# One zero fill moved behind the w_down stores and gate/up loads in five FFN blocks

## Chip, cores and metric

The kernel runs on one core of a Trainium2 chip. Its time is the device time of that core in microseconds, as the median of several executions; below, profiles give a span of one execution, which starts with the first instruction and is a little shorter.

## What is computed

The kernel computes one decode step of a transformer block, forward and backward. `c` gives six modulation vectors; `x` goes through a modulated layer norm, attention over the last 4096 positions of a long cache, a second modulated layer norm and a gated FFN. The outputs are the new `x` and the gradients of all inputs.

```python
W = min(4096, max(256, Sk // 4))          # Sk is 65536
k = jnp.repeat(k_cache[:, :, Sk - W:, :], rep, axis=1)
v = jnp.repeat(v_cache[:, :, Sk - W:, :], rep, axis=1)
...
h = _sigmoid(g) * u
return jnp.einsum('bsf,fd->bsd', h, w_down)
...
x = x + gb * _B_ref(h, B_w_gate, B_w_up, B_w_down)
```

Two of the gradients, those of `k_cache` and `v_cache`, have the shape of the whole cache (4 x 65536 x 128 each). Only their last 4096 positions are not zero, so the rest has to be filled with zeros in device memory. That is most of what the kernel writes.

## The kernel before

The kernel is written out by hand in one order (`manual_schedule`), and each engine runs its own instructions in that order. Work goes in stages: load the modulation weights and the cache, attention forward, the matrices that the attention gradients need, the FFN, and at last all the gradients that hang on the FFN's result.

**The zero fills.** The zero region of the two cache gradients is cut into pieces of [128, 4096] elements, 1 MB each. `zero(n)` (L147 on) takes the next n of them off a list and issues each as one DMA from GpSimd (L169; a few narrower ones are issued in two parts, L162 and L165). A fill has no input but a tile of zeros that stays in SBUF, so it can be placed anywhere. The tables at the head of the file (`Z_...`) say how many fills go to which place; they are spread over the whole kernel, among the transfers that carry data.

**Queues.** GpSimd issues the fills, the stores of weight gradients and the loads of the gate and up weights, all through one software queue (q0 in the profile), and waits at each for what that transfer depends on. A GpSimd DMA also takes one of eight semaphores in turn, so it waits for the landing of the eighth GpSimd DMA before it. SyncE issues the loads of w_down through a queue of its own (q1).

**The FFN.** F = 3584 is done in `NB` = 7 blocks q of 512 columns. A block holds the gate and up weights in a tile of two halves (j = 0 to 3 and 4 to 7), double buffered by q % 2, and w_down in one tile `wd_v` of two halves s. In block q:

- VectorE, for each j, multiplies the weights by the gradient of gate/up and sums (`ttr`, L210, into `dh2acc`), and ScalarE overwrites the same tile with the weight gradient (`outer_act`, L241). In between PE and ScalarE transpose pieces of w_o and v for later (`side`, L836 and L837).
- After j = 3 the first half of the weight gradient is stored (`store_ug(q, 0, 4)`, L868, two DMAs of 512 KB), after j = 7 the second half (`store_ug(q, 4, 4)`).
- Then PE and ScalarE compute the gate and up values of block q + 1 (`front`, `gates`), VectorE reduces its two w_down halves (`wd_ttr`, L210 into `junk`) and overwrites them with the gradient (`wd_outer`, L206), which is stored from the same place (`store_wd`, L854).
- `load_ug(q + 2, ...)` (L864) fetches the gate/up weights of block q + 2 into the half that `store_ug(q, ...)` has emptied, so it waits for that store's landing. `load_wd(q + 2, s)` (L851, SyncE) likewise waits for the landing of `store_wd(q + 1, s)`, and `wd_ttr(q + 2, s)` waits for the load.
- At the end of the block `dug_part` (L989, L990) makes the gradient of gate/up for the next block.

`Z_FFN` has four numbers per block: fills after the first gate/up store, after the second, after the first w_down store (and the first load), and after the second load.

Of the kernel before, what the change touches and what calls it, by code (L numbers as in the profile page):

```python
# [52 lines left out]
Z_N = spread(31, 128)  # L53
Z_B = [n + (i in (31, 38)) for i, n in enumerate(spread(29, 43))] + [1, 1, 1, 1, 0] + [1, 1, 0, 1, 1, 0, 1, 1] + [1, 0, 1, 0, 1, 0, 0, 0]
Z_FOLD = (1, 1, 3)
Z_FFN = [(1, 1, 0, 1)] * 5 + [(1, 1, 1, 2), (1, 2, 1, 0)]
Z_END = (1, 2, 1, 0, 0)
@with_exitstack
def kernel(
# [956 lines left out]
    for q in range(NB):  # L1016
        z = Z_FFN[q]
        more = q + 1 < NB
# [315 lines left out]
```

## Time and profile before

| what | value |
|---|---|
| time, median of 3 | 599.43 us (599.01 to 601.42) |
| profiled span | 598.7 us |
| bytes by DMA | 246.64 MB, of which HBM written 185.60 MB and read 60.30 MB |
| busiest engine | PE 411.2 us (69%), then VectorE 326.6, ScalarE 284.9, GpSimd 163.1 |
| DMA | 9 tenths busy in all slices but the first (8) and the last (6) |
| the FFN | about 319 to 480 us, one block some 22 to 25 us |

Read it from the DMA row: the sixteen DMA engines hardly rest. The time of a span can only fall if fewer bytes move, if they move faster, or if a stretch in which too little was queued is filled. For a change of order, look at single stretches of the FFN: the GB/s of each, what GpSimd waits for before an issue, and how long VectorE waits for a w_down load.

### The profile page before, as it was taken

To read this page: it belongs to the slowest core of one execution; us is meant where nothing else is said; L and a number is where in the kernel's file an instruction comes from. 1 tells how busy PE (TensorE), PEld (TensorE's weight loads), DVE (VectorE), ACT (ScalarE), POOL (GpSimd) and SP (SyncE) were. 2 spreads that over 40 slices of the span, in tenths; PEclk is the share of its full clock that TensorE was granted. 3 is DMA by queue.
4 is the path that set the end of the run, shared out by engine and by line. 5 is a ranking of instruction groups with operands and counts; after the bars stand their busy time and mean duration, and the time that the engine had idled before them with its cause. 6 is when DMAs were issued, how large, how long until landed. Compare 5 with 4: busy or idle time off the path is not lost.

```text
span 598.7 us, 11068 instructions
## 1 busy us (share of the span) xinstructions
PE 411.2 (69%) x4612; PEld 275.3 (46%) x4612; DVE 326.6 (55%) x620; ACT 284.9 (48%) x429; POOL 163.1 (27%) x262
## 2 busy tenths in 40 slices
PE   3997689999999989999984435534445196766300
PEld 3995334334344545546664334433344166565300
DVE  3654499999511010160007495694777888768530
ACT  2489514567211014213225665864867866873200
POOL 0003123222223212222232244333343253122330
PEclk9999699999999999999995555555555586755555
DMA  8999999999999999999999999999999999999996
GB/s 349 419 418 422 413 425 412 427 421 425 427 419 426 422 428 423 422 421 424 423 397 407 421 411 415 411 411 412 379 403 412 424 416 414 420 424 425 424 415 269
DMA packets 45027, 246.64 MB, mean 412 GB/s; under 512 B 5085, under 2 KB 5085, under 8 KB 24544
## 3 DMA queue, kind: packets, MB, share of 16 engines
q0 software_dynamic: 38832, 216.55, 94.7%
q1 hardware_dynamic: 6096, 29.37, 12.5%
q8 instruction: 36, 0.59, 0.4%
q14 instruction: 15, 0.12, 0.1%
q10 hardware_dynamic: 48, 0.01, 0.0%
HBM read 60.30 MB, written 185.60 MB: 411 GB/s over the span
## 4 chain that ended last, share of the span: by engine, by line
PE 40%; DMA 26%; DVE 19%; ACT 7%; issue 4%; ACTq 0%; POOLq 0%; SPq 0%; DVEq 0%
PE b_ps L691 17%; DMA out_dram<-arena 16%; DMA arena<-in_B_w_down_dram 6%; PE n_ps L636 6%; DVE junk L210 5%; DVE arena L210 4%; DVE arena L193 4%; DVE arena L206 4%; DMA arena<-in_B_w_gate_dram 3%; ACT arena L241 3%; PE t_ps L598 2%; PE tp_wq L453 2%; PE w_ps L394 2%; PE tp_k L434 1%; PE fold_ps L875 1%
## 5 line engine op out<-in xcount | busy, mean ns | idle before, releaser
L169 POOL DMA_DIRECT2D out_dram<-zeros x114 | 62.0, 545 | 200.4 <-PE q_ps L471 50.7
L691 PE MATMUL b_ps<-arena 128*128 128x512 bf16 x512 | 116.2, 379 | 0.0
L836 PE MATMUL tp_side<-ident_bf,arena 128*128 128x128 bf16 x432 | 51.7, 300 | 46.6 <-ACT arena L837 39.7
L837 ACT COPY arena<-tp_side 128x1024 bf16<-128x1024 bf16 x54 | 53.9, 1012 | 50.7 <-PE tp_side L836 50.4
L193 DVE TENSOR_TENSOR arena<-arena 128x2048 bf16<-128x2048 bf16 x64 | 76.5, 1223 | 2.3 <-PE n_ps L636 0.3
L691 PEld LDWEIGHTS <-arena 128*128 128x128 bf16 x512 | 48.8, 98 | 55.8 <-issue 2.9
L210 DVE CUSTOM_DVE_ANT_0 arena<-arena,scr 128x1024 bf16<-128x1024 bf16 x56 | 65.2, 1219 | 10.4 <-ACT scr L990 10.4
L636 PE MATMUL n_ps<-arena 128*128 128x512 bf16 x256 | 65.7, 378 | 6.2 <-DVE arena L193 4.6
L836 PEld LDWEIGHTS <-arena 128*128 128x128 bf16 x432 | 43.0, 139 | 51.2 <-issue 50.9
L241 ACT ACTIVATE arena<-scr,h 128x1024 bf16<-128x1024 bf16 x56 | 61.5, 1146 | 1.4 <-DVE dh2acc L210 1.3
L636 PEld LDWEIGHTS <-arena 128*128 128x128 bf16 x256 | 24.6, 97 | 41.6 <-issue 16.2
L210 DVE CUSTOM_DVE_ANT_0 junk<-arena,b1k 128x1024 bf16<-128x1024 bf16 x28 | 34.2, 1222 | 10.1 <-DMA arena<-in_B_w_down_dram 9.6
L1161 ACT ACTIVATE arena<-ps_kv 128x512 bf16<-128x512 f32 x48 | 26.1, 680 | 26.8 <-PE ps_kv L1157 26.5
L868 POOL DMA_DIRECT2D out_dram<-arena x28 | 21.1, 760 | 63.9 <-ACT arena L241 44.9
L202 DVE CAST arena<-b_ps 128x512 bf16<-128x512 f32 x6 | 4.1, 691 | 61.6 <-PE b_ps L691 61.6
L600 ACT CAST arena<-t_ps 128x512 bf16<-128x512 f32 x56 | 30.1, 589 | 12.1 <-PE t_ps L598 12.1
L1157 PE MATMUL ps_kv<-junk,arena 8*128 8x128 bf16 x256 | 27.1, 303 | 10.9 <-DVE arena L206 9.5
L1157 PEld LDWEIGHTS <-arena 8*128 8x128 bf16 x256 | 25.1, 139 | 12.6 <-issue 12.6
L455 ACT COPY arena<-tp_wq 128x1024 bf16<-128x1024 bf16 x23 | 21.8, 1032 | 8.1 <-PE tp_wq L453 8.1
L970 PE MATMUL fg<-hh_bf,arena 128*128 128x1 bf16 x224 | 8.2, 166 | 20.7 <-DMA arena<-in_B_w_down_dram 17.8
L877 ACT CAST arena<-fold_ps 128x512 bf16<-128x512 f32 x16 | 9.4, 588 | 24.1 <-PE fold_ps L875 24.1
L655 ACT ACTIVATE arena<-n_ps 128x512 bf16<-128x512 f32 x8 | 4.3, 594 | 33.1 <-PE n_ps L652 33.1
(299 smaller groups left out, 652.8 us busy)
## 6 DMA issues: line engine op xcount, KB each, us to landing
out_dram<-zeros POOLq DMA_DIRECT2D x114, 1024.0 KB, 14.6
out_dram<-arena POOLq DMA_DIRECT2D x32, 1024.0 KB, 17.1
out_dram<-arena POOLq DMA_DIRECT2D x50, 512.0 KB, 9.7
arena<-in_A_wq_dram SPq DMA_DIRECT2D x8, 1024.0 KB, 20.4
arena<-in_A_wo_dram POOLq DMA_DIRECT2D x8, 1024.0 KB, 11.9
arena<-in_w_mod_dram POOLq DMA_DIRECT2D x7, 1024.0 KB, 18.1
arena<-in_B_w_down_dram SPq DMA_DIRECT2D x14, 512.0 KB, 8.9
arena<-in_B_w_up_dram POOLq DMA_DIRECT2D x14, 512.0 KB, 9.9
```

Of the source, the lines that this page charges most:

```text
L169: ins = nc.gpsimd.dma_start(out=region.bitcast(FP32), in_=zeros[:, :])
L193: return nc.vector.tensor_tensor(out=out, in0=a, in1=b, op=op)
L206: return nc.vector.tensor_scalar(out=out, in0=a, scalar1=s1, scalar2=None, op0=op0)
L210: return nc.vector.tensor_tensor_reduce(out=out, in0=w, in1=b, scale=1.0, scalar=0.0, op0=ALU.mult, op1=ALU.add, accum_out=acc)
L241: return nc.scalar.activation(out=out, in_=b, func=ACT.Copy, scale=col)
L600: nc.scalar.copy(out=o, in_=ps)
L636: mm = nc.tensor.matmul(nbank[k][:, :], lhsT=k_nat[:, g, t_ * DH:(t_ + 1) * DH], rhs=vp[:, t_ % 2, 4 * k:4 * k + 4, :].rearrange("p h d -> ...
L691: mm = nc.tensor.matmul(bbank[p][k][:, :], lhsT=a4[:, p, h, :], rhs=wo_t[u][:, a, k * 512:(k + 1) * 512], start=(i == 0 and a == 0), stop= ...
L836: nc.tensor.transpose(tp[:, i * P:(i + 1) * P], blk[:, i * P:(i + 1) * P], ident_bf[:, :])
L837: nc.scalar.copy(out=blk if dst is None else dst, in_=tp[:, :])
L1157: nc.tensor.matmul(ps[:, t4 * DH:(t4 + 1) * DH], lhsT=rows[32 * g:32 * g + HG, t_ * P:(t_ + 1) * P], rhs=hd[32 * g:32 * g + HG, :], start= ...
L1161: nc.scalar.activation(out=o, in_=ps[:, :], func=ACT.Copy, scale=float(scale))
```

## The change

In blocks 0 to 4, the fill that stood after the second gate/up store is issued at the end of the block instead, behind the w_down stores and the loads of gate and up, where one fill stood already. It brings those stores and loads forward in GpSimd's queue by one fill, and leaves two fills in a row before the next block's first store. Blocks 5 and 6 and the number of fills stay.

```diff
-Z_FFN = [(1, 1, 0, 1)] * 5 + [(1, 1, 1, 2), (1, 2, 1, 0)]
+Z_FFN = [(1, 0, 0, 2)] * 5 + [(1, 1, 1, 2), (1, 2, 1, 0)]
```

The order of GpSimd's DMAs in one of these blocks:

```
before   store A   zero   store B   zero   load A   store w0   store w1   load B   zero
after    store A   zero   store B          load A   store w0   store w1   load B   zero   zero
```

(A and B are the halves of the gate/up tile, w0 and w1 those of w_down.)

## Prediction

> **What bounds the kernel now.** I read the page's DMA rows first, then the stage table, then the chain of waits, then GpSimd's timeline around the moved fill.
>
> ```profile
> DMA packets 45027, 246.64 MB, mean 412 GB/s; under 512 B 5085, under 2 KB 5085, under 8 KB 24544
> q0 software_dynamic: 38832, 216.55, 94.7%
> q1 hardware_dynamic: 6096, 29.37, 12.5%
> ```
>
> These are the page's DMA rows. All 40 slices but the first and the last stand at 9 tenths of DMA time, and no compute engine is above 69%. 246.64 MB in 598.7 us is a kernel that waits for transfers. Nearly all of them go through q0, which GpSimd fills in program order; q1 (SyncE) carries the w_down loads in the stage concerned.
>
> The stage table (columns: stretch in us, its length, busy us of PE, PEld, DVE, ACT and POOL, clock, DMA share, GB/s) has a stretch long before the FFN, then the FFN in steps of 23 us, about one block each:
>
> ```profile
> 160.00:280.00 120.00, 115.61 (x885) 60.82 (x883) 22.88 (x57) 24.16 (x35) 28.91 (x51) 1.00 1.13 423
> 343.00:366.00 23.00, 10.40 (x160) 8.88 (x158) 16.18 (x35) 16.31 (x18) 9.60 (x14) 0.50 1.07 413
> 366.00:389.00 23.00, 11.40 (x168) 9.80 (x166) 17.02 (x37) 16.23 (x18) 8.66 (x14) 0.50 1.07 412
> 389.00:412.00 23.00, 9.63 (x138) 8.08 (x136) 15.12 (x32) 16.45 (x18) 8.93 (x14) 0.50 1.07 409
> 412.00:435.00 23.00, 10.28 (x160) 9.10 (x160) 16.08 (x31) 14.34 (x15) 7.44 (x11) 0.50 1.10 392
> 435.00:458.00 23.00, 10.91 (x163) 9.39 (x161) 16.36 (x35) 17.32 (x22) 9.00 (x13) 0.50 1.06 406
> ```
>
> The FFN moves 409 to 413 GB/s in ordinary blocks, and less in two. The finer windows say where:
>
> ```profile
> 420.00:424.00 4.00, 2.05 (x16) 1.73 (x17) 2.60 (x10) 1.55 (x3) 2.48 (x4) 0.50 0.99 382
> 424.00:428.00 4.00, 1.32 (x12) 1.15 (x12) 4.00 (x7) 4.00 (x5) 0.16 (x1) 0.50 0.98 324
> 428.00:432.00 4.00, 0.99 (x11) 0.83 (x10) 3.90 (x8) 4.00 (x5) 1.98 (x3) 0.50 1.11 415
> ```
>
> That is the only real hole: (412-382)/412 x 4 + (412-324)/412 x 4 = 0.29 + 0.85 = 1.1 us.
>
> The chain of waits, in order of time, shows why compute was late there:
>
> ```profile
> 369.84 10.08 DMA out_dram<-arena
> 379.98 7.70 DMA arena<-in_B_w_down_dram
> 405.01 12.62 DMA arena<-in_B_w_down_dram
> 417.65 1.22 DVE junk L210
> ```
>
> A w_down store has to land before the next w_down load may use its tile; that load has to land before VectorE goes on. Here one load took 12.62 us against 7.70, VectorE started only at 417.65, and the next gate/up store came so late that the queue thinned. The loop of store, load, compute is in the chain, yet DMA runs at its usual rate in every other block: it has about the length of the block's transfers and does not limit by itself.
>
> **What the Trainium skill says.** "DMA: Bandwidth & Descriptors", section "Issuing engines are not separate DMA queues": all DMAs share 16 engines and interleave. The trace agrees: total GB/s stays near 412 while q1 runs beside q0. The same page, section "Queues, rings and completion order", says each engine takes its queues in turn by packets, and "Anatomy of one DMA — SWDGE (gpsimd) path" says the engines never wait on semaphores; the issuing sequencer does, and holds all behind it. The trace agrees with that too: GpSimd's issues stand in program order with gaps before those that wait for ACT, VectorE or a landing. No page gives a price for fill order.
>
> **The change, part by part.** Call the halves of a gate/up store A and B, the loads into the same halves U and V, the w_down stores w0 and w1, a 1 MB fill Z. One block on GpSimd was A Z B Z U w0 w1 V Z; it becomes A Z B U w0 w1 V Z Z. No instruction of PE, ACT, VectorE or SyncE changes, and fills keep their order, so none is added or lost.
>
> 1. Bytes. Per block A, B, U and V move 1 MB each, the w_down stores 1 MB, the w_down loads 1 MB on q1, fills 3 MB: 9 MB (9.44e6 bytes) at 412 GB/s is 22.9 us. Unchanged, so the floor under a block is unchanged.
>
> 2. GpSimd time. Fills cost 545 ns each on GpSimd (the row of L169). The same number is issued: 0.
>
> 3. The fill removed from behind B. U waits for A's landing, V for B's. A's place in the stream is unchanged: two fills follow V before the next A where one did, but one fewer stood earlier. So U is issued when it was. What has changed is what lies in q0 while GpSimd stands there: Z and B, 2 MB or 5.1 us, instead of 3 MB and 7.6 us. In the profile U's two issues stand at 391.69 and 392.89 with 2.56 and 0.44 us of wait before them. 5.1 us is still more than the longest such wait (4.5 us, once). Cost: 0, with up to 5.1 - 4.5 = 0.6 us of slack left.
>
> 4. U, w0, w1, V sit one fill earlier in q0. 1.05 MB / 412 GB/s = 2.5 us sooner each. The w_down loads hang on w0 and w1, so they start up to 2.5 us sooner. VectorE waits 9.6 us in five times for these loads (3.8 at most), so nearly all of each early wait goes. But this is compute time, hidden: from one copy of dug (422.6) to the next (444.5) a block without such waits takes 21.9 us of compute, and its transfers 22.9. Compute reaches the end of the FFN some 2.5 us earlier; the bytes do not. Worth 0 directly.
>
> 5. Two fills behind V, ahead of the next A. A waits for ACT's first half of outer products; this is the place of the hole (V and its fill issued by 423.6, A at 430.02). The fill adds 2.5 us of queued work exactly there, more than the 1.1 us lost, and step 4 makes A's data come sooner. Gain up to 1.1 us. The next stretch (406 against 412: 0.3 us) may gain as well.
>
> 6. Overlap. A w_down load now runs beside V, Z, Z rather than V, Z, A. If fills take a larger share than stores do, the load lasts longer; between the quick and the slow loads of the chain (7.70 and 12.62 us) lies 4.9, most of which is the one bad case. I take 1 us, covered by the 2.5 of step 4.
>
> Sum: 0 to -1.4 us. The slow load at 405 may be an accident of this one execution (DMA share rises to 1.39 just then, in one window of 4 us), so I take -0.8: 599.4 - 0.8 = 598.6 us.
>
> **The rivals.**
> - Hidden (599.4 us): the hole belongs to the profiled execution, or comes back elsewhere. For it: the transfer total is unchanged and the queue full in four of six stretches. Against it: the added fill sits just where the queue thinned.
> - Faster (about 594.3 us): the order itself lifts the rate, as loads and stores lie closer and compute is no longer late. If the 138 us of the FFN (mean 407 GB/s of the six stretches from 320 to 458) ran at the 423 of the stretch before, 138 x (1 - 407/423) = 5.2 us. Half of that, 2.6 us, is short of 0.5%. Against it: even the undisturbed blocks, with full queues, show 409 to 413, so the mix of transfers sets the rate, and the mix stays.
> - Slower (about 603.7 us): the thinner queue behind B runs dry while GpSimd stands at U or V, and w0 waits behind them. A hole like that at 424 (0.85 us) in each of five blocks is 4.3 us. The extreme, the full 2.5 us each time, is 12.7. For it: GpSimd stood 7.0 us in three waits at such loads for landings. Against it: A normally lands after about 9 to 10 us in a queue, that is, with B behind it already issued, so data is there to move.
>
> **How the numbers follow.** Forecast (-0.3 to -1.5 us): 0.50. Hidden, within about 1 us of before: 0.25. Faster by over 3 us: 0.12. Slower by over 3 us: 0.13. Both of the first two lie within 0.5% (596.4 to 602.4), so same is 0.75. The range 595.5 to 602.3 takes in them, half a gain of rate, and the cheaper holes; the tails outside hold 2 in 10 or less.
>
> **What would show it.** Right: in the changed profile the two last stretches of the FFN stand at 409 to 413 GB/s, no 4 us window at 324; VectorE's waits for in_B_w_down fall from 9.6 us to under 4; the copy of dug before the last block comes some 2.5 us before 465.35; DMA bytes 246.64 MB. Wrong to the slow side: windows below 380 GB/s just after a B store, with GpSimd standing at L864. Wrong to the fast side: ordinary blocks well above 413 GB/s. If VectorE's waits stay, step 4 is wrong; if they go and a hole of the same size stays before A, step 5 is.

## Result and profile after

The changed kernel takes 603.4 us (median of 6) against 599.5: ratio 1.0064, 95% interval 1.0044 to 1.0084. Run again beside two of the experiments it came to 603.9, ratio 1.0073 (1.0051 to 1.0095). It is slower by 4 us, outside the stated range, and close to the time of the third rival.

The profiled execution has a span of 603.1 us. Bytes and packets are the same, the rate is not (page, DMA rows):

```profile
DMA packets 45027, 246.64 MB, mean 409 GB/s; under 512 B 5085, under 2 KB 5085, under 8 KB 24544
q0 software_dynamic: 38832, 216.55, 94.3%
q1 hardware_dynamic: 6096, 29.37, 12.7%
```

The stage table of the FFN, columns as before (the last is GB/s):

```profile
343.00:366.00 23.00, 10.53 (x160) 9.21 (x160) 16.09 (x31) 14.58 (x15) 8.18 (x12) 0.50 1.13 365
366.00:389.00 23.00, 10.79 (x162) 9.36 (x160) 16.58 (x37) 17.32 (x22) 9.08 (x14) 0.50 1.07 406
389.00:412.00 23.00, 10.57 (x160) 9.13 (x160) 16.11 (x32) 15.68 (x17) 8.65 (x13) 0.50 1.07 406
412.00:435.00 23.00, 10.65 (x160) 9.20 (x160) 16.39 (x34) 16.27 (x21) 9.73 (x14) 0.50 1.07 398
435.00:458.00 23.00, 10.26 (x159) 9.07 (x160) 16.39 (x34) 15.37 (x19) 9.11 (x13) 0.50 1.06 397
```

Before, they stood at 413, 412, 409, 392 and 406. Now every one is below 412, most of all the first; only the fourth, where before had its hole, is higher than it was. A second profile of the changed kernel (after_again, below; the slowest of its executions too) has 376, 387, 395, 389 and 394 there. Finer windows find the thin places:

```profile
352.00:356.00 4.00, 1.75 (x16) 1.42 (x15) 2.67 (x6) 2.61 (x3) 2.63 (x5) 0.50 0.84 277
420.00:424.00 4.00, 1.75 (x16) 1.42 (x15) 2.65 (x6) 2.20 (x3) 2.17 (x4) 0.50 1.02 343
424.00:428.00 4.00, 1.90 (x16) 1.58 (x15) 4.00 (x9) 4.00 (x5) 1.55 (x3) 0.50 1.02 395
448.00:452.00 4.00, 1.76 (x15) 1.43 (x14) 4.00 (x9) 4.00 (x5) 1.41 (x3) 0.50 1.04 355
```

At 424 to 428, where before stood at 324 GB/s, after stands at 395. The thin places are now where GpSimd issues the w_down stores and V, or just behind. GpSimd's timeline of the block from 369 us (start, length, line, transfer, in brackets the idle time before it and what ended that):

```profile
370.60 0.76 POOL L864 DMA_DIRECT2D arena<-in_B_w_up_dram  x1 [2.11 <-DMA out_dram<-arena]
371.91 0.75 POOL L864 DMA_DIRECT2D arena<-in_B_w_gate_dram  x1 [0.55 <-issue]
372.65 0.56 POOL L854 DMA_DIRECT2D out_dram<-arena  x1
374.18 0.56 POOL L854 DMA_DIRECT2D out_dram<-arena  x1 [0.97 <-DVE arena L206]
375.70 0.77 POOL L864 DMA_DIRECT2D arena<-in_B_w_up_dram  x1 [0.97 <-DMA out_dram<-arena]
377.01 0.77 POOL L864 DMA_DIRECT2D arena<-in_B_w_gate_dram  x1 [0.54 <-issue]
377.77 1.12 POOL L169 DMA_DIRECT2D out_dram<-zeros  x2
```

Loads of gate and up (L864) are issued one by one as the halves of A and B land: by the landing records A at 370.04 and 371.35, B at 375.09 and 376.40. Each load is issued some 0.6 us after the landing that it waits for. The waits that the profile puts down to these landings are three times as long as before. First before, then after (us in total, times, longest):

```profile
POOL arena L864 <- DMA out_dram<-arena: 7.0, 3, 4.5
```

```profile
POOL arena L864 <- DMA out_dram<-arena: 21.2, 10, 4.4
```

The labels overstate this growth. GpSimd's idle time before these loads under all labels (PE and "issue" as well) is 19.3 us before and 29.0 after, half as much again. By the landing records, 12 of the 20 single loads were issued 0.6 us after the landing of their store already before, and 16 in after; the issues at 391.69 and 392.89 of before, whose waits the profile puts down to PE, followed landings at 391.09 and 392.29.

From issue and landing records one can count what GpSimd has issued and what has not landed when U or V is issued: before 3.5 MB nearly everywhere (3.0 at two V), after 2.5 MB in most, and 1.5 at V in block 0. (MB of 2^20 bytes, as for the sizes of the fills.) That is what the prediction's own order says: behind the half of A that still flies (0.5 MB) lie Z and B, no second Z. The DMA issues between 340 and 452 us (KB each, median us to landing) show the other side; first before, then after:

```profile
arena<-in_B_w_up_dram POOLq DMA_DIRECT2D x10, 512.0 KB, 9.5
arena<-in_B_w_down_dram SPq DMA_DIRECT2D x10, 512.0 KB, 8.2
```

```profile
arena<-in_B_w_up_dram POOLq DMA_DIRECT2D x10, 512.0 KB, 7.5
arena<-in_B_w_down_dram SPq DMA_DIRECT2D x9, 512.0 KB, 10.4
```

A load of gate/up lands sooner, because less is ahead of it, but not sooner by the whole fill: 2.0 us, not 2.5. The w_down load takes 2.2 us longer.

### The profile page after: what moved, and what is told of

It reads as the page before. It is cut to its first block, busy times and chain, and to the rows that moved or that the text cites. A ratio compares the mean times of both kernels' runs of the same rounds, so it can differ in the third digit from the quotient of the medians.

```text
span 603.1 us, 11067 instructions
## 1 busy us (share of the span) xinstructions
PE 411.1 (68%) x4612; PEld 275.4 (46%) x4612; DVE 326.5 (54%) x620; ACT 284.7 (47%) x429; POOL 165.2 (27%) x262
## 4 chain that ended last, share of the span: by engine, by line
PE 40%; DMA 29%; DVE 16%; ACT 6%; issue 4%; POOL 0%; ACTq 0%; POOLq 0%; SPq 0%; DVEq 0%
PE b_ps L691 17%; DMA out_dram<-arena 15%; DMA arena<-in_B_w_down_dram 8%; PE n_ps L636 6%; DMA arena<-in_B_w_gate_dram 5%; DVE arena L210 4%; DVE arena L193 4%; DVE arena L206 4%; PE t_ps L598 2%; DVE junk L210 2%; ACT arena L241 2%; PE w_ps L394 2%; PE tp_wq L453 2%; PE tp_k L434 1%; ACT arena L837 1%
## 5 line engine op out<-in xcount | busy, mean ns | idle before, releaser
L691 PEld LDWEIGHTS <-arena 128*128 128x128 bf16 x512 | 48.8, 98 | 55.8 <-issue 2.9
L836 PEld LDWEIGHTS <-arena 128*128 128x128 bf16 x432 | 42.9, 139 | 50.4 <-issue 50.1
L636 PEld LDWEIGHTS <-arena 128*128 128x128 bf16 x256 | 24.6, 97 | 41.6 <-issue 16.2
L970 PEld LDWEIGHTS <-arena 128*128 128x128 bf16 x224 | 7.3, 105 | 28.8 <-DMA arena<-in_B_w_down_dram 26.9
```

Source lines behind the costliest of these rows:

```text
L636: mm = nc.tensor.matmul(nbank[k][:, :], lhsT=k_nat[:, g, t_ * DH:(t_ + 1) * DH], rhs=vp[:, t_ % 2, 4 * k:4 * k + 4, :].rearrange("p h d -> ...
L691: mm = nc.tensor.matmul(bbank[p][k][:, :], lhsT=a4[:, p, h, :], rhs=wo_t[u][:, a, k * 512:(k + 1) * 512], start=(i == 0 and a == 0), stop= ...
L836: nc.tensor.transpose(tp[:, i * P:(i + 1) * P], blk[:, i * P:(i + 1) * P], ident_bf[:, :])
```

## Experiments

Names: T1, too little is queued while GpSimd stands at U or V. T2, two fills in a row slow the w_down loads, and compute is late. T3, only the first block counts. T4, w_down stores stand on GpSimd behind waiting loads. Each time is the median of 4 to 22 executions; each ratio is to the kernel before, run beside it, with its 95% interval.

| run | order in blocks 0 to 4 | us | ratio |
|---|---|---|---|
| before | A Z B Z U w0 w1 V Z | 599.4 to 599.8 | 1 |
| after_again | A Z B U w0 w1 V Z Z | 603.9 | 1.0073 (1.0051 to 1.0095) |
| x_2001 | A Z Z B U w0 w1 V Z | 600.2 | 1.0015 (1.0006 to 1.0023) |
| x_0102 | A B Z U w0 w1 V Z Z | 601.3 | 1.0044 (1.0028 to 1.0059) |
| x_1011 | A Z B U w0 Z w1 V Z | 600.5 | 1.0017 (1.0009 to 1.0025) |
| x_block0 | after in block 0 alone | 599.7 | 1.0009 (1.0000 to 1.0017) |
| x_blocks14 | after in blocks 1 to 4 alone | 601.6 | 1.0039 (1.0027 to 1.0051) |
| t3_before | before, three buffers | 600.0 | 1.0010 (0.9999 to 1.0022) |
| t3_after | after, three buffers | 600.3 | 1.0020 (1.0009 to 1.0031) |
| st_before | before, still tile | 600.3 | 1.0014 (1.0007 to 1.0021) |
| st_after | after, still tile | 600.5 | 1.0020 (1.0008 to 1.0033) |
| sp_before | before, w stores on SyncE | 599.2 | 0.9997 (0.9988 to 1.0006) |
| sp_after | after, w stores on SyncE | 600.9 | 1.0033 (1.0019 to 1.0048) |
| w0_first | A Z B w0 U w1 V Z Z | 601.4 | 1.0033 (1.0021 to 1.0045) |
| x_0003 | A B U w0 w1 V Z Z Z | 613.8 | 1.0237 (1.0224 to 1.0250) |
| x_1200 | A Z B Z Z U w0 w1 V | 602.3 | 1.0048 (1.0036 to 1.0060) |
| x_1102 | A Z B Z U w0 w1 V Z Z | 604.3 | 1.0072 (1.0047 to 1.0097) |

**Where the fill stands, and in which block.** One table line each:

```diff
-Z_FFN = [(1, 1, 0, 1)] * 5 + ...
+Z_FFN = [(2, 0, 0, 1)] * 5 + ...                     x_2001
+Z_FFN = [(0, 1, 0, 2)] * 5 + ...                     x_0102
+Z_FFN = [(1, 0, 1, 1)] * 5 + ...                     x_1011
+Z_FFN = [(1, 0, 0, 2)] + [(1, 1, 0, 1)] * 4 + ...    x_block0
+Z_FFN = [(1, 1, 0, 1)] + [(1, 0, 0, 2)] * 4 + ...    x_blocks14
```

> Blocks 0 to 4: A Z Z B U w0 w1 V Z (the fill from behind B goes ahead of B, one fill at the end as before). Theory T1 (too little is queued between a half's store and the load into the same half: behind A lie 3.5 MB when U is reached as before, behind B only 2.5 MB when V is reached as after): about half the loss, 601 to 602 us. Rival T2 (two fills in a row at the end slow the w_down loads, so compute and the next A are late): one fill at the end, so as before, 599.5.

> Blocks 0 to 4: A B Z U w0 w1 V Z Z (the fill behind A goes to the end, the one behind B stays). T1: behind A 2.5 MB, behind B 3.5 MB: about half the loss, 601 to 602 us; with the run that has 2 0 0 1 it shows which half counts. T2: two fills at the end: the whole loss, 603.4.

> Blocks 0 to 4: A Z B U w0 Z w1 V Z (the fill from behind B goes between the w_down stores). T1: 2.5 MB behind A, 3.5 MB behind B, and w1 one fill later: 601 to 602 us. T2: one fill at the end: 599.5.

> The change in block 0 alone, blocks 1 to 4 as before. In the profile of after, block 0's end (348 to 362 us) has the deepest hole, about 2.8 of some 5.7 us lost below 412 GB/s. T1: every block loses, this one most: 600.5 to 601.5 us. Rival T3 (only the first block, where a w_down load came late, counts): the whole loss, 603.4.

With one of the two places thin and one fill at the end the loss is 0.7 to 1.0 us, about a quarter of the whole: less than T1 had said and more than T2's nothing. x_0102, with two at the end, has its median where T1 had it, 601.3, but its runs fall into one group at 601.1 to 601.3 and one at 602.9 to 604.1, near T2's 603.4. These runs did not decide between T1 and T2. Block 0 alone costs next to nothing by the median, which ends T3; T1's forecast (600.5 to 601.5) missed it too.

The upper group is at least in part another matter. The profile of x_0102 is of its slowest execution. In it a load of modulation weights landed late, ahead of the FFN: the first w_down store was issued at 326.18 us (before: 319.32), and 318 to 332 us moved 353 GB/s (before: 405), ahead of the first store of block 0, where all these kernels have the same order. The profiles of after_again (325.46 us, 367 GB/s) and x_0003 (325.67, 364) show the same. Against 405 GB/s, 1.3 to 1.8 us of each are lost there. How many of the other executions have it is not known.

**Taking either wait away.** Three buffers take the landing of A and B out of U's and V's waits; the still tile takes the landing of the w_down store out of the w_down load's.

```diff
-    ug_v = arena[:, 16 * KIB:48 * KIB].rearrange("p (h q j k f) -> p q h j k f", h=2, q=2, j=4, k=2)
+    ug_b = [[ar(o, 8).rearrange("p (j k f) -> p j k f", j=4, k=2) for o in pair]
+            for pair in ((16, 32), (24, 40), (128, 136))]                    # used by q % 3
...
-        nc.gpsimd.dma_start(out=wd_dram(out_8, q, s), in_=wd_v[:, 2 * s:2 * s + 2, :])
+        dep(nc.gpsimd.dma_start(out=wd_dram(out_8, q, s), in_=still[:, 2 * s:2 * s + 2, :]), after)
```

(The first pair of lines is t3, the second st; `still` is an arena tile that nothing overwrites, `after` the outer product that the store waited for.)

> Order of before, but the gate/up tiles are rotated over three buffers instead of two, so that no load of gate/up waits for the landing of the store just before it. The third buffer lies over the folded modulation weights, so the part of the gradient of c that comes from them is computed from other data. T1 (the wait of U for A and of V for B): no or little gain over before, 598.5 to 599.5. T2 (late w_down loads): the same.

> Order of after with the same three buffers (the same part of the gradient of c is computed from other data). T1: U and V no longer wait for A and B, so the loss goes: within 1 us of the three-buffer run in the order of before. T2 (two fills in a row slow the w_down loads and make compute late): the w loop is untouched, so the loss stays, 602 to 603.5.

> Order of before, but the w_down stores send another tile that nothing overwrites, at the same places and after the same VectorE instructions, so that the w_down loads wait for VectorE alone and not for a landing. The gradient of w_down is computed but not what is stored. T1: hardly changed, 598.5 to 599.5. T2: at most the hole of before goes, 598 to 599.5.

> Order of after with the same still tile for the w_down stores (the gradient of w_down is computed but not what is stored). T1: U and V still wait for A and B with 2.5 MB queued behind, so most of the loss stays: 601.5 to 603.5. T2: the w_down loads come early and compute is never late for them, so the loss goes: within 1 us of the order of before.

With three buffers after is 0.3 us behind before, well within the intervals: T1's forecast held, T2's failed. With the still tile the gap is 0.2, and there T1's forecast failed and T2's held: U and V still found 2.5 MB. (Both kernels in the order of before took 0.6 to 0.9 us longer than before itself, where 599.5 at most was forecast.) The queues of the window 370 to 378 us, in which U, w and V are issued in both (packets, MB, share), first after, then st_after, tell why:

```profile
q0 software_dynamic: 775, 3.15, 103.0%
```

```profile
q0 software_dynamic: 586, 2.17, 69.7%
q1 hardware_dynamic: 288, 1.05, 32.9%
```

In after the thin place has q0 alone; the w_down loads run later, beside the fills. Freed of the store's landing, they come just then, and 1.05 MB on q1 fill in. In the same 8 us of the other four blocks (24 us apart) st_after has 0.78 to 1.05 MB on q1 and 400 to 407 GB/s, after nothing on q1 and 360 to 395. So what counts would be the bytes on both queues. That reading came after the fact, and only these windows stand behind it.

**T4: the w_down stores behind U.**

```diff
-        nc.gpsimd.dma_start(out=wd_dram(out_8, q, s), ...
+        nc.sync.dma_start(out=wd_dram(out_8, q, s), ...        # sp_before, sp_after
...
             if q + 2 < NB:
                 load_ug(q + 2, 0, 4)
-            wd_outer(q + 1, 0)                                 # w0_first: this call first
```

> Order of before, with the w_down stores issued by SyncE on its own queue instead of GpSimd, so that no w_down store stands behind a load of gate/up. T4 (the three-buffer and the still-tile runs each took most of the loss away, so the loss needs both loops: w_down stores stand on GpSimd behind loads that wait for A, the w_down load is then late, and so is the compute that makes the next A): 598.5 to 599.5 us, the DMA rate being the limit. T1 (too little queued in GpSimd's queue between store and load): only 2.5 MB then lie behind A1 and B1 less the w_down stores, so slower, 600 to 602.

> Order of after with the w_down stores on SyncE's queue. T4: nothing stands behind U any more that the next w_down load needs, so the loss goes: within 1 us of the same edit in the order of before. T1: U and V wait as in after, with still less in GpSimd's queue behind A and B (2.5 and 1.5 MB): 603.5 or more.

> Order of after, but the first w_down store is issued ahead of U instead of behind it: A Z B w0 U w1 V Z Z in blocks 0 to 4. T4: w0 no longer stands behind U's wait: most of the loss goes, 600 to 601.5. T1: U is issued later still, behind VectorE's outer product, and no more is queued: 603 or more.

> The change in blocks 1 to 4 alone, block 0 as before. Block 0 alone cost 0.2 us. If the blocks add up, 603.2. If the loss has to build up over consecutive blocks (T4: each late A makes the next loads late), it is near that of the whole change too, 602.5 to 603.2; if the first block sets it off, about 600.

Each edit removed about half of the loss and left 1.8 to 1.9 us (sp_after is 1.8 behind sp_before). T1 missed all three times; T4 had sp_before and, just, w0_first in its ranges, and missed sp_after, where the loss was to go. Both edits also change what is queued: w0_first puts 3.0 MB behind most U instead of 2.5, sp_after puts the w_down stores beside V on q1. They left T4 possible as a part. In block 0 of after its route can be seen: a w_down load took 14.73 us (before: 10.06), the w_down store behind it waited 4.50 us for VectorE, and V, behind that store, was issued 3.1 us after B had landed, with 1.5 MB left. x_blocks14 with 2.1 and x_block0 with 0.2 make 2.3, not 4, and none of the three forecasts of x_blocks14 held.

**How much is queued.**

```diff
-Z_FFN = [(1, 1, 0, 1)] * 5 + ...
+Z_FFN = [(0, 0, 0, 3)] * 5 + ...     x_0003
+Z_FFN = [(1, 2, 0, 0)] * 5 + ...     x_1200
+Z_FFN = [(1, 1, 0, 2)] * 5 + ...     x_1102
```

> The changed kernel itself, on the same chip as the two runs beside it, so that the parts can be set against the whole: 603.4 us as first measured; if it is nearer 602, the parts (block 0 alone 0.2, blocks 1 to 4 alone 2.1) add up.

> All three fills of blocks 0 to 4 at the end: A B U w0 w1 V Z Z Z. Behind A1 lie 1.5 MB when U is reached, behind B1 2.5 MB when V is. If the amount queued while GpSimd stands at a load sets the loss (T1), it grows clearly: 606 us or more. If only the place of the w_down stores behind U counts (T4), U's wait for A starts when it did and the w_down stores come one more fill sooner: about as after, 602 to 604.

> The other way: A Z B Z Z U w0 w1 V, no fill at the end. Behind A1 and B1 lie 4.5 MB, so GpSimd hardly stands at a load. T1: no loss there, but nothing fills the stretch before the next A, and the w_down stores are one fill later: 599.5 to 602. If the fill at the end had been worth what the prediction gave it (up to 1.1 us per thinning, in one block), at least 600.5.

> A Z B Z U w0 w1 V Z Z in blocks 0 to 4: the two fills at the end of after, and the fill behind B of before as well. The five fills come from the stages after the FFN, which have none left. If the missing fill behind B is the cause (3.5 MB behind A1 and B1 again), the FFN stretches are back at 409 to 413 GB/s each, and the time is that of before give or take what the later stages lose without their fills, 599 to 602 us. If the two fills in a row at the end are the cause (later w_down loads), the FFN stretches stay below 406 as in after, 602 or more.

x_0003 has 1.5 MB at most U and loses 14 us, three and a half times as much as 2.5 MB (in its profile 1.4 us of that are lost ahead of block 0). T4 had said 602 to 604 and falls as the main cause. Two of its stretches:

```profile
389.00:412.00 23.00, 7.99 (x94) 6.78 (x93) 16.51 (x34) 13.37 (x16) 8.92 (x13) 0.50 1.00 361
412.00:435.00 23.00, 9.71 (x153) 8.23 (x151) 14.11 (x31) 13.10 (x16) 7.37 (x11) 0.50 1.00 357
```

x_1102 puts back the fill behind B and keeps two at the end. Its FFN:

```profile
343.00:366.00 23.00, 9.84 (x143) 8.31 (x141) 15.62 (x35) 16.22 (x18) 10.15 (x15) 0.50 1.08 412
366.00:389.00 23.00, 10.84 (x160) 9.23 (x160) 16.38 (x34) 15.66 (x18) 8.88 (x13) 0.50 1.08 414
389.00:412.00 23.00, 8.12 (x93) 6.86 (x93) 16.08 (x31) 13.12 (x14) 8.69 (x14) 0.50 1.11 414
500.00:520.00 20.00, 13.61 (x321) 12.80 (x319) 16.06 (x45) 13.58 (x20) 7.91 (x11) 0.67 1.01 376
```

The thin places are gone (the two later FFN stretches have 406 and 409), although GpSimd stands longer at the loads than before or after (34.7 us under all labels), and VectorE longer for w_down than in any other run here. The landings alone:

```profile
POOL arena L864 <- DMA out_dram<-arena: 28.2, 8, 6.8
```

```profile
DVE junk L210 <- DMA arena<-in_B_w_down_dram: 18.1, 8, 4.2
```

So neither these waits nor the two fills in a row cost the FFN any rate as long as 3.5 MB are queued, and T2 falls as the main cause. (Each block also has a fill more than in the other orders. What that does by itself was not tried.) Its time is no better than after's, because the five fills are missing later: 376 GB/s at 500 to 520 us, in the stage without fills (before: 418). As T1 had it the rate of the FFN came back (four of five stretches in its 409 to 413 or above), but the loss in the later stages was larger than the forecast of the time allowed for.

x_1200 has 4.5 MB at most U and V and waits little for landings (4.7 us in two waits), but with no fill at the end it thins ahead of and around the next A (373 and 365 GB/s at 380 to 388 us, in its fastest execution) and loses 2.6 us, slightly more than T1's range. Both ends of the block need a fill; of the orders tried with three fills a block, before has the best split. sp_before is no faster that can be told (0.9988 to 1.0006).

## Why the prediction was wrong

- **What bounds it: right.** DMA is the limit and bytes are unchanged; in the profile of after all of the loss is lower GB/s in the FFN.
- **Step 3 is the one that failed.** It saw that behind A only 2 MB (5.1 us) would lie where 3 had lain (7.6), and priced that at nothing since GpSimd's longest such wait had been 4.5 us. That compares the wrong two things. A was taken to land when it did, and GpSimd to have a margin in its wait; but U is issued 0.6 us after A's landing, however long GpSimd stood, and what has to last from then, until U's own bytes follow, is what is behind A. The loss went with that amount and not with the wait: x_1102 has a wait of 6.8 us and keeps its rate with 3.5 MB queued, x_0003 shows 1.5 MB costing 14 us. So the price of the thinner queue, put at 0, was some 4 us. An estimate of the size: 2.5 MB at 412 GB/s are 6.4 us, and such a load lands after 7.5; before, 3.5 MB are 8.9 and it lands after 9.5. The difference, 0.5 us for each of ten pairs of loads, is 5 us; measured were 4. One execution does not spread it so evenly: below 412 GB/s, the five stretches of after lose 2.6, 0.3, 0.3, 0.8 and 0.8 us.
- **The third rival** named this mechanism and a time of 603.7, by taking the size of the hole at 424 for each block. It was given 0.13 on the ground that B was already issued when A landed. It was; it was not enough. Its sign came true (windows at 277 and 343 GB/s with GpSimd at L864). That its time fits so well is in part luck: the losses are uneven, and the hole whose size it took is not one of the order, as step 5 shows.
- **Step 4 failed.** The w_down stores do land sooner after their issue (7.7 us in the median against 9.6), but VectorE's waits for w_down did not go:

```profile
DVE junk L210 <- DMA arena<-in_B_w_down_dram: 13.0, 6, 5.3
```

  They were 9.6 us before, and 9.3 in the profile of after_again; forecast was under 4. Compute came later, not 2.5 us earlier: the copy of dug before the last block stands at 468.42 us (before: 465.35).
- **Step 5: a gain that was hardly there to be had.** The window went from 324 to 395 GB/s, but the hole was one of the profiled execution. x_block0 has the order of before in this block and none:

```profile
412.00:435.00 23.00, 11.10 (x174) 9.57 (x175) 16.76 (x35) 16.22 (x18) 9.00 (x14) 0.50 1.07 412
424.00:428.00 4.00, 1.01 (x8) 0.84 (x8) 4.00 (x7) 4.00 (x5) 0.45 (x1) 0.50 1.04 409
```

  The second profile of the changed kernel has 349 GB/s in the same window. The prediction had said that the slow load ahead of the hole might be an accident, and took the gain in all the same. x_1200 shows what it costs to have no fill there; a second one was not worth what the place behind B lost.
- **Step 6: too small.** The w_down load became 2.2 us longer, not 1. By the t3_after run, where it still took some 9.9, this alone costs little there.

Not settled: why block 0 alone costs 0.2 and blocks 1 to 4 alone 2.1, when together it is 4 (the profile of x_block0 has 388 GB/s in the first stretch, 1.3 us below 412), and why one thin place costs less than half of two. The profiled execution of after is the slowest of its six, with an extra hole in block 0 (277 GB/s), so its shares by block are not those of the median.

Nor is it shown what the DMA engines do in a thin place. At 352 to 356 us of after fewer than 16 data packets were under way for 70% of the time, so there not all 16 engines had work. At 420 to 424 (343 GB/s) that was so for 10% only: the 4 KB packets took 193 ns in the mean against 168 at 376 to 380 (406 GB/s), with the median hardly changed (165 and 159), since 21 of them took over 0.3 us against 2. The runs show that the rate falls with what is queued behind the store, not by which way.

## What to carry to other kernels

Where a load reuses the buffer of a store, count the bytes queued, on all DMA queues, between that store and the load behind it: here they had to last from the store's landing until the load's bytes followed, and a fill was worth more there than as a second one at the end of the block. A long wait on the issuing engine did no harm to the rate with 3.5 MB queued; shorter ones went with a loss at 2.5 MB. A profile's label for a wait can hide what it waited for; landing times tell. Before a hole in one profile is counted as a gain, look for it in a second execution. Filler that only moves is not free even in a kernel bound by bytes: its two places have to be priced both, the one it leaves first.

## Not expected of the hardware

In several runs bursts of 4-byte packets on SyncE's queue took 1.6 to 2.2 us each in the packet records (9 ns in the median): nine between 412 and 416 us of before, just where its w_down load took 12.62 us, and sixteen between 342 and 346 us of after, ahead of its deepest hole. They come with either order and in different blocks: sp_before, no slower than before, has over twenty in the FFN. Their cause was not tried.
